# An attention and feed-forward kernel on one core: its thousand work items in a new order

## The chip, the cores and the metric

The kernel runs on one core of a Trainium2 chip. The metric is device time in microseconds, the median of several runs, lower is better. Profiles are of one execution each. The engines are TensorE (PE in the profile; its weight loads are PEld), VectorE (DVE), ScalarE (ACT), GpSimd (POOL) and SyncE (SP), which here only issues transfers.

## The reference

Four sequences of 768 tokens, eight heads of 64. Heads 0, 2 and 6 ("retrieval") attend causally to everything before them; the other five ("streaming") attend to the first 4 tokens and to a window of 64. Then a two-layer feed-forward block with a leaky rectifier follows.

```python
scores = scale * np.matmul(q, k.transpose(0, 1, 3, 2))
causal = rel >= 0                       # rel: query position minus key position
stream_keep = causal & (is_sink | in_win)   # sink: key < 4; window: rel < 64
a = softmax of scores, masked by causal (retrieval) or stream_keep (streaming)
x = (a @ v), heads side by side         # 3072 tokens x 512
h = x @ w_in                            # 512 -> 2048
g = np.maximum(h, 0.0) + alpha * np.minimum(h, 0.0)
out = g @ w_out                         # 2048 -> 512
```

## The kernel before

**Segments and items.** A segment `n` (0 to 15) is one pair of heads of one sequence: sequence `n // 4`, pair `n % 4` of (2,6), (1,5), (0,4), (3,7). The feed-forward block works in tiles `t` (0 to 7): even ones are the first 512 tokens of a sequence, odd ones the other 256. All work is cut into a thousand named items, and the list `ORDER` says in which order they are emitted. Every engine, and every queue that issues transfers, executes its own instructions strictly in that order; an instruction that waits holds up all behind it on its engine. So the list is the whole schedule: no planner stands between it and the chip.

**Names.** Of segment `n`, head `h` (0 or 1), part `m`:

- `Lq`, `Lk`, `Lv`: loads of q, k and v, issued on SP (the first half of `Lk0` on ScalarE's queue). There are four buffers of each, so `Lk10` must wait for the cast of segment 6.
- `Cq`, `Ck`, `Cv`: casts to bf16; on GpSimd for segments 0 to 5, on ScalarE or VectorE later (`Cq6` and `Cq7` on ScalarE, `Cv6` on VectorE). `Cv` of a streaming pair in the first sequence has two small copies behind the cast.
- `T`, `t`: transposes of q and k by TensorE (L361, L363) and their copy out of PSUM to `qT`, `kT` (L368, L386 to L394), segments 0 to 7. From segment 8 on, `Dq` and `Dk` do both with transposing transfers on SP.
- `S`, `s`, `m`: score matmuls (L413; L423 and L430 from segment 4 on), exp by ScalarE (L469, L517 to L523), mask by VectorE (L479, L528, L531). The first sequence adds its masks on TensorE instead (L462, L501). Some `m` items hold no instruction.
- `A`, `a`: products with v (L552), normalized by VectorE (L562, L563). `X`, `x`: the transpose of that into `xT`, on TensorE for segments 0 to 3 and 15, else as a transposing transfer on SP (L571).
- `P`, `p`, `g`: up-projection of a tile (L597), `relu(-h)` by ScalarE (L602), the leaky rectifier by VectorE (L609). Some `P0` items are cut in three, so that they can start before all four segments are there.
- `O`, `o`: a quarter of a down-projection (four matmuls, L617), its copy by ScalarE (L623) and the store (L627, on GpSimd's queue for tiles under 6, else SP). The very last 128 tokens are cut by columns: `L0` to `L2` and `l0` to `l2` (L636, L645, L646).
- `wi0` to `wi7` and `wo0` to `wo3`: pieces of the two weights, issued by GpSimd (L692, L696). `wi0` and `wi1` together hold the first 512 columns of `w_in`, `wi6` and `wi7` the last.
- `warm0` to `warm8`: filler matmuls on zeros (L687), 32, 3, 14 and then 4 each. The rest (`id`, `kz`, `sz`, `nms`, `ns`, ...) fill constants and masks.

**Banks.** PSUM has eight banks. An item that needs one takes the free one that was given back longest ago, as the list is read; so the order also decides whose copy a matmul waits for.

**Bursts.** From segment 4 on, score matmuls are collected while only items follow that may stand beside them (casts, copies, exps, loads). When another item comes, the collected ones are issued. If both heads have at least 576 columns, the matmuls of the two heads alternate, each with its 64 rows of keys and queries (L430), and run beside each other on the two halves of the array; otherwise they are issued one by one with all 128 rows, of which half are zeros (L423):

```python
if min(columns) < SPLIT:                 # 576
    for x in burst:
        nc.tensor.matmul(*x[3:6], start=True, stop=True)
else:
    ...
```

Of the kernel before, what the change touches and what calls it, by code (L numbers as in the profile page):

```python
# [14 lines left out]
busy zero La id warm0 kz3 Lq0.0 sz1 vz2 nms nmr so1 vz0 Lq0.1 Lk1 warm8 warm5 warm3 kz1 qz0 one Lq1 Lk0 Ck0.0 Cq0.0  # L15
Tq0.0 tq0.0 Tk0.0 qz kz0 kz2 idf warm2 Lk2 tk0.0 Ck1.0 Ck1.1 Cq0.1 Tk1 S0.0.1 s0.0.1 Tq0.1 S0.0.0 Cq1 warm7 Lv0 tk1.0
sz2 vz1 vz3 Tq1 Lq2 Ck0.1 S0.0.2 s0.0.0 tk1.1 Tk0.1 Ck2.1 tq1 S1.1.0 s0.0.2 Ck2.0 warm4 tq0.1 nz0 s1.1.0 Cq2 tk0.1 Cv0
Lk3 S0.1.0 kfz0 Lv1 vo ro0 Ck3.1 s0.1.0 Lq3 Ck3.0 wi1 wi0 Cq3 sz0 S1.0.0 so2 Al s1.0.0 so0 al S0.1.1 s0.1.1 Lv2 Tq2
Tk2 tk2.1 tk2.0 S0.1.2 S1.0.1 A0.0 s0.1.2 a0.0 Cv1 A0.1 a0.1 Cv2 s1.0.1 tq2 S1.1.1 nz1 Tk3 S2.0.1 tk3.0 s1.1.1 S2.0.2
X0 s2.0.1 x0 wi6 s2.0.2 wi7 Lv3 Lq5 Tq3 tk3.1 S2.0.0 wi5 m4.0.2 warm6 S2.1.0 A1.0 a1.0 Lk4 s2.0.0 A2.0 S2.1.1 A1.1  # L20
a2.0 tq3 s2.1.0 a1.1 S3.0.0 s2.1.1 s3.0.0 A2.1 a2.1 S3.1.1 X1 S3.0.1 s3.0.1 Lk5 wi4 kfz2 Cv3.0 Cq5 Lk7 wi2 X2 Ck4.0
s3.1.1 S3.1.0 x1 P0.0.0 x2 P0.0.1 A3.0 P0.1.0 P0.1.1 Lk6 Lq4 Lq6 Ck4.1 kfz3 nr Cv3.1 s3.1.0 A3.1 Lv7 Lv5 Lq7 Ck5.0 wi3
# [824 lines left out]
```

## Time and profile before

| | before |
|---|---|
| median of 3 runs | 229.27 us (229.27 to 230.81) |
| the profiled execution | 229.83 us |
| its span, first to last instruction | 228.0 us |
| TensorE busy | 222.4 us, 2005 matmuls |
| VectorE, ScalarE, GpSimd busy | 151.6, 139.6, 45.8 us |
| transfers | 37.39 MB, mean 164 GB/s |

The page names for each group its line, engine, what it writes and reads, how often it occurs, and the mean time of one. "Idle before" is time that the engine stood ahead of such instructions, with what ended most of it. Matmuls are pipelined: their busy times overlap, so the distance from one start to the next says what each costs. The chain that ended last goes back from the last instruction to what released each step.

### The profile page before, as it was taken

The page shows a single profiled execution, that of the slowest core. Times are in us where ns is not written, and L with a number is a line of the kernel's source. Part 1 is how long each engine was busy: PE and PEld are TensorE (multiplying, and loading weights), DVE is VectorE, ACT ScalarE, POOL GpSimd, SP SyncE. Part 2 cuts the span into 40 slices and gives each one's busy share as a digit, 9 for nine tenths or more (in the row PEclk, how much of TensorE's full clock was granted, in tenths as well). Part 3 has the DMA queues.
Part 4 walks back from the last instruction along what each step waited for, and adds up shares of the span by engine and source line. Part 5 has one row for each costly group of instructions (what it writes and reads, how often), then busy time and mean ns, then how long its engine had stood idle before and what let it go on. Part 6 is the DMA issues. An engine that isn't in the chain of part 4 may idle for free.

```text
span 228.0 us, 5239 instructions
## 1 busy us (share of the span) xinstructions
PE 222.4 (98%) x2005; PEld 135.9 (60%) x2005; DVE 151.6 (66%) x395; ACT 139.6 (61%) x284; POOL 45.8 (20%) x91
## 2 busy tenths in 40 slices
PE   8999999999999999999999999999999999999994
PEld 8789876563455656555556455556556555664454
DVE  7769849966389816899699219987586535966000
ACT  2689559999799128477994136787594236563311
POOL 6769996101130001000400001000110110000000
PEclk9999999999999999999999999999999999999999
DMA  6999999999998798989969899995821420000213
GB/s 190 313 229 210 286 223 262 206 197 241 206 287 142 132 204 227 172 192 181 254 153 199 194 266 146 218 166 107 132 93 38 116 95 0 0 4 0 88 66 123
DMA packets 95417, 37.39 MB, mean 164 GB/s; under 512 B 82440, under 2 KB 93600, under 8 KB 95392
## 3 DMA queue, kind: packets, MB, share of 16 engines
q1 hardware_dynamic: 89136, 27.73, 61.2%
q0 software_dynamic: 5792, 8.93, 17.1%
q10 hardware_dynamic: 464, 0.40, 0.5%
q8 instruction: 15, 0.25, 0.5%
q14 instruction: 10, 0.08, 0.2%
HBM read 27.71 MB, written 6.29 MB: 149 GB/s over the span
## 4 chain that ended last, share of the span: by engine, by line
PE 92%; ACT 3%; DVE 2%; issue 1%; DVEq 0%; ACTq 0%
PE P L597 35%; PE P L617 34%; PE P L552 7%; PE P L430 4%; PE P L687 3%; PE P L413 2%; PE P L363 2%; PE P L636 2%; ACT neg L602 1%; PE P L501 1%; DVE kT L392 1%; PE P L423 1%; PE P L577 1%; ACT kT L392 1%; ACT eS L523 1%
## 5 line engine op out<-in xcount | busy, mean ns | idle before, releaser
L609 DVE SCALAR_TENSOR_TENSOR g<-neg,oma,P 128x256 bf16<-128x256 f32 (+1 forms) x128 | 71.0, 608 | 35.9 <-ACT neg L602 35.5
L597 PE MATMUL P<-xT,w_in_b 128*128 128x512 bf16 (+1 forms) x512 | 86.5, 326 | 0.0
L617 PE MATMUL P<-w_out_b,g 128*128 128x512 bf16 x368 | 85.4, 379 | 0.0
L602 ACT ACTIVATE neg<-P 128x512 f32<-128x512 f32 x96 | 54.4, 600 | 27.2 <-PE P L597 22.6
L597 PEld LDWEIGHTS <-w_in_b 128*128 128x128 bf16 x512 | 49.5, 98 | 31.7 <-DVE g L609 0.2
L617 PEld LDWEIGHTS <-g 128*128 128x128 bf16 x368 | 33.8, 98 | 37.2 <-issue 1.2
L469 ACT ACTIVATE eR<-P 128x448 bf16<-128x448 f32 (+4 forms) x63 | 37.1, 636 | 5.4 <-PE P L430 2.3
L623 ACT COPY ot<-P 128x512 f32<-128x512 f32 x23 | 13.8, 602 | 37.8 <-PE P L617 32.9
L627 POOL DMA_DIRECT2D out_dram<-ot x18 | 10.3, 571 | 113.2 <-ACT ot L623 113.0
L517 ACT ACTIVATE eS<-P 128x352 bf16<-128x352 f32 x45 | 21.0, 493 | 3.7 <-PE P L430 3.7
L563 DVE TENSOR_TENSOR xn<-P,rcp 128x448 bf16<-128x448 f32 (+1 forms) x32 | 19.5, 608 | 1.1
L528 DVE TENSOR_TENSOR eS<-eS,ms_near 128x352 bf16<-128x352 bf16 x45 | 14.3, 334 | 4.4 <-ACT eS L517 4.2
L479 DVE TENSOR_TENSOR eR<-eR,mr_near 128x128 bf16<-128x128 bf16 (+5 forms) x54 | 12.1, 252 | 4.0 <-ACT eR L469 4.0
L430 PE MATMUL P<-qT,kT 64*128 64x176 bf16 (+13 forms) x181 | 11.7, 251 | 0.3 <-DVE g L609 0.3
L430 PEld LDWEIGHTS <-kT 64*128 64x128 bf16 x181 | 7.2, 94 | 7.6 <-issue 6.8
L413 PE MATMUL P<-qT,kT 128*128 128x192 bf16 (+14 forms) x68 | 11.3, 251 | 0.3 <-ACT eS L523 0.3
L552 PE MATMUL P<-vb,eS 128*128 128x65 bf16 x260 | 11.0, 193 | 0.4 <-DVE eS L528 0.4
L552 PEld LDWEIGHTS <-eS 128*128 128x128 bf16 x260 | 9.7, 97 | 2.9 <-DVE eS L528 0.6
L562 DVE RECIPROCAL rcp<-P 128x7 f32<-128x7 f32 (+1 forms) x32 | 6.3, 198 | 7.1 <-PE P L552 6.9
L552 PE MATMUL P<-vb,eR 128*128 128x65 bf16 x276 | 10.1, 192 | 0.0
L552 PEld LDWEIGHTS <-eR 128*128 128x128 bf16 x276 | 9.4, 97 | 1.2
L645 DVE COPY ot<-P 128x128 f32<-128x128 f32 x1 | 0.3, 292 | 14.3 <-PE P L636 14.3
(95 smaller groups left out, 175.5 us busy)
## 6 DMA issues: line engine op xcount, KB each, us to landing
out_dram<-ot POOLq DMA_DIRECT2D x18, 256.0 KB, 3.6
kf<-in_k_dram SPq DMA_DIRECT2D x21, 192.0 KB
qf<-in_q_dram SPq DMA_DIRECT2D x18, 192.0 KB
vf<-in_v_dram SPq DMA_DIRECT2D x14, 196.0 KB
qf<-in_q_dram SPq DMA_DIRECT2D x7, 384.0 KB
vf<-in_v_dram SPq DMA_DIRECT2D x12, 192.0 KB
w_in_b<-in_moe_w_in_dram POOLq DMA_DIRECT2D x8, 256.0 KB, 9.7
w_out_b<-in_moe_w_out_dram POOLq DMA_DIRECT2D x4, 512.0 KB, 13.4
```

The lines of the kernel that those rows point to most:

```text
L413: nc.tensor.matmul(to, keys, queries, start=True, stop=stop)
L430: nc.tensor.matmul(to, keys[own], queries[own], start=True, stop=True)
L469: nc.scalar.activation(ebuf[n, hh][:, lo:hi].rearrange("p (x c) -> p x c", x=len(parts)), P[:, got[0]:got[0] + len(parts), 0:(hi - lo) // ...
L517: nc.scalar.activation(slots, sc[:, 0:352].rearrange("p (s c) -> p s c", c=176), AF.Exp, scale=scale)
L528: nc.vector.tensor_tensor(slots, slots, ms_near[:, 0:2, :] if m == 0 else ms_near[:, 1:3, :], op=ALU.mult)
L552: nc.tensor.matmul(pav[:, i, :], e[:, o:o + 128], vv[:, j, hh, 0:D + 1], start=(m == 0), stop=(m == len(terms) - 1))
L563: nc.vector.tensor_tensor(xn[n][:, 0:nt, D * hh:D * hh + D], pav[:, :, 0:D], rcp.to_broadcast([128, nt, D]), op=ALU.mult)
L597: nc.tensor.matmul(psg[:, w * i:w * (i + 1)], w_in_b[:, c, 128 * fb:128 * (fb + 1)], xT[:, c, o:o + w], start=(x == 0), stop=(x == 3))
L602: nc.scalar.activation(neg[t, f], bank(held["P", t, f][0]), AF.Relu, scale=-1.0)
L609: nc.vector.scalar_tensor_tensor(g_buf[t % 2][:, fb, 0:w], neg[t, f][:, c], oma[:, fb:fb + 1], bank(got[0])[:, c], op0=ALU.mult, op1=ALU.add)
L617: nc.tensor.matmul(bank(held["O", t, s][0]), g_buf[t % 2][:, f, 128 * s:128 * (s + 1)], w_out_b[:, f, :], start=(f == 0), stop=(f == 15))
L623: nc.scalar.copy(ot, bank(got[0]))
```

## The change

Only the list `ORDER` changes. It holds the same items, each once, in another order over its whole length; no function and no constant is touched. Which score matmuls are collected into one burst, and which banks the items take, follow from the new order. Of the 56 lines on each side the diff below shows the opening, the middle around segments 4 to 7, the end of the second batch in the new list, and the end.

```diff
--- before
+++ after
 ORDER = """
-busy zero La id warm0 kz3 Lq0.0 sz1 vz2 nms nmr so1 vz0 Lq0.1 Lk1 warm8 warm5 warm3 kz1 qz0 one Lq1 Lk0 Ck0.0 Cq0.0
-Tq0.0 tq0.0 Tk0.0 qz kz0 kz2 idf warm2 Lk2 tk0.0 Ck1.0 Ck1.1 Cq0.1 Tk1 S0.0.1 s0.0.1 Tq0.1 S0.0.0 Cq1 warm7 Lv0 tk1.0
-sz2 vz1 vz3 Tq1 Lq2 Ck0.1 S0.0.2 s0.0.0 tk1.1 Tk0.1 Ck2.1 tq1 S1.1.0 s0.0.2 Ck2.0 warm4 tq0.1 nz0 s1.1.0 Cq2 tk0.1 Cv0
-Lk3 S0.1.0 kfz0 Lv1 vo ro0 Ck3.1 s0.1.0 Lq3 Ck3.0 wi1 wi0 Cq3 sz0 S1.0.0 so2 Al s1.0.0 so0 al S0.1.1 s0.1.1 Lv2 Tq2
-Tk2 tk2.1 tk2.0 S0.1.2 S1.0.1 A0.0 s0.1.2 a0.0 Cv1 A0.1 a0.1 Cv2 s1.0.1 tq2 S1.1.1 nz1 Tk3 S2.0.1 tk3.0 s1.1.1 S2.0.2
-X0 s2.0.1 x0 wi6 s2.0.2 wi7 Lv3 Lq5 Tq3 tk3.1 S2.0.0 wi5 m4.0.2 warm6 S2.1.0 A1.0 a1.0 Lk4 s2.0.0 A2.0 S2.1.1 A1.1
-a2.0 tq3 s2.1.0 a1.1 S3.0.0 s2.1.1 s3.0.0 A2.1 a2.1 S3.1.1 X1 S3.0.1 s3.0.1 Lk5 wi4 kfz2 Cv3.0 Cq5 Lk7 wi2 X2 Ck4.0
-s3.1.1 S3.1.0 x1 P0.0.0 x2 P0.0.1 A3.0 P0.1.0 P0.1.1 Lk6 Lq4 Lq6 Ck4.1 kfz3 nr Cv3.1 s3.1.0 A3.1 Lv7 Lv5 Lq7 Ck5.0 wi3
...
-m4.1.3 A5.0 a5.0 X5 s4.1.1 A4.0 s7.0.0 s7.1.1 Lk11 Lq8 s7.0.1 a4.0 s6.0.5 near1 m7.0.0 m7.1.1 m4.1.0 O1.1.0 S7.1.0
-S6.0.4 S7.0.2 S4.1.5 S6.0.1 S7.1.2 S6.1.1 O1.1.1 Cv6 s7.1.0 O1.0.0 s4.1.5 m7.0.1 s6.1.1 m4.1.5 m6.1.1 s7.1.2 m6.1.0
-s7.0.2 m7.0.2 S6.0.2 S4.1.2 S6.1.2 S6.0.0 s6.0.4 s4.1.2 s6.0.1 s6.1.2 O1.0.1 m6.0.5 m7.1.0 m4.1.1 m4.1.4 m7.1.2 m6.1.2
...
-O0.0.1 O0.0.2 O1.0.2 m10.0.2 O1.0.3 O0.0.3 o0.0 X4 X6 a7.1 a7.0 X7 P2.9 P2.3 p2.9 P3.4 Ck9 Cq9 g2.9 P2.14 p2.14 g2.14
-Cq8 p3.4 Lq10 Lq11 Dk8.0 P2.10 p2.10 Dk9.1 o1.0 p2.3 g2.3 g3.4 Dk8.1 P3.2 P3.14 P3.12 P2.8 Dq8 P2.1 P3.8 o1.1 p3.2
...
-g3.0 p2.15 g2.7 g2.15 S8.0.0 p2.12 g2.12 Ck11 p3.6 S9.0.2 P2.6 p2.6 g3.6 s8.0.0 p2.4 g2.4 g2.6 s9.0.2 p3.8 P3.10 g3.8
-p3.10 O3.0.0 O2.0.0 S8.1.5 s8.1.5 O3.0.1 O2.0.1 g3.10 m8.0.0 Cv8 S8.1.3 S9.0.0 S8.0.3 S9.1.1 S8.0.1 S9.1.0 s8.1.3
-s9.1.0 s8.0.1 s9.0.0 s8.0.3 m8.0.3 m8.0.1 O2.0.2 O2.0.3 o2.0 Dk10.1 Lv9 m9.0.0 Cv9 m8.0.5 Dk11.0 m9.1.0 m9.0.2 S8.0.4
...
-p6.14 g6.14 g7.12 O6.3.3 o6.3 O6.0.2 O6.1.2 O6.1.3 o6.1 O6.0.3 o6.0 O6.2.0 O6.2.1 O6.2.2 O7.0.1 O7.0.2 O6.2.3 o6.2
-m12.0.2 g7.14 L2 l2 O7.0.3 o7.0 L0 L1 l1 warm1 l0
+id vo kz3 busy warm0 sz0 vz0 zero nms warm5 nz1 nmr sz1 Lq0.0 so1 kz1 Lk1 qz0 Lq1 Cq0.0 Lq0.1 sz2 Ck1.0 Lk0 Ck0.0
+Tq0.0 La Ck1.1 Cq1 Cq0.1 tq0.0 Lk2 Ck2.0 Tk0.0 kz0 Lv0 warm2 Ck0.1 ro1 Ck2.1 Tk1 tk0.0 S0.0.1 S0.0.0 Tq1 Lq2 tk1.0 Cv0
+s0.0.1 Cq2 Tq0.1 Lk3 tk1.1 nz0 Lq5 Lq3 m4.1.2 so2 warm4 S0.0.2 tq0.1 warm7 warm6 Tk0.1 m8.1.2 s0.0.0 tq1 qz S1.1.0 Tk2
+Ck3.1 Ck3.0 s0.0.2 vz1 Lv1 tk0.1 vz3 S0.1.0 idf s1.1.0 Cq3 kz2 tk2.1 warm3 S1.0.0 warm8 s0.1.0 Al al tk2.0 s1.0.0
+S0.1.1 vz2 Lv2 Tq2 s0.1.1 S0.1.2 s0.1.2 wi1 wi0 tq2 A0.0 a0.0 S1.1.1 A0.1 s1.1.1 Lv3 S1.0.1 a0.1 Cv1 Cq5 Cv2 Tk3 tk3.1
+s1.0.1 wi7 Lk4 S2.0.1 s2.0.1 S2.0.2 so0 Lk5 X0 x0 Tq3 S2.0.0 wi6 tk3.0 s2.0.2 A1.0 A1.1 a1.0 S2.1.1 wi5 wi4 Cv3.0
+s2.0.0 a1.1 Tq5 ro0 S2.1.0 tq3 A2.0 a2.0 s2.1.1 S3.1.1 Ck4.0 wi2 s2.1.0 A2.1 s3.1.1 S3.0.0 Ck4.1 S3.0.1 X1 s3.0.1 one
...
+P0.9 Tk6 kfz1 p0.4 g0.4 O0.2.0 Cv5 p0.9 P0.5.0 tk6.1 m5.1.1 tk6.0 P1.8 P0.5.1 P0.5.2 p0.5 g0.9 S5.1.0 g0.10 s5.1.0
+Ck7.1 g0.5 Tq6 tq6 S4.0.2 m5.1.0 s4.0.2 p0.8 g0.8 P1.6 p1.6 g1.6 O0.1.0 Tk7 tk7.1 O0.3.0 O0.3.1 Cv6 p1.8 tk7.0 O0.1.1
+S5.0.2 S5.1.2 S4.0.4 S6.1.0 s5.1.2 s5.0.2 s6.1.0 s4.0.4 m4.0.1 O0.1.2 O0.1.3 m4.0.4 Cv4 o0.1 near0 g1.8 S4.1.0 S4.1.4
+S4.0.3 S4.0.0 Cq7 O0.2.1 s4.1.4 O0.2.2 m5.1.2 Tq7 s4.0.0 s4.0.3 m4.0.5 tq7 m4.0.3 O0.2.3 o0.2 A5.1 a5.1 Lk8 S5.0.1
+s5.0.1 s4.1.0 O0.3.2 O0.3.3 o0.3 Lk9 S4.1.1 S6.0.4 S7.1.1 S6.0.5 Lq9 S4.1.3 S4.1.5 S6.0.0 near2 m4.1.4 s7.1.1 m5.0.1
...
+m4.1.1 m12.0.2 s7.0.2 Lk11 S6.1.2 s6.1.2 m6.1.2 S4.1.2 O1.0.0 m6.0.0 m7.0.2 S6.0.2 s4.1.2 Dk8.1 O1.0.1 m6.1.0 s6.0.1
+m6.0.1 s7.1.2 m7.1.2 A4.1 a4.1 S7.0.0 A6.1 a6.1 s6.0.2 Lq8 A6.0 a6.0 S7.0.1 s7.0.1 X4 A7.1 m7.0.1 O1.1.2 O1.1.3 X6
+m8.0.2 s7.0.0 m7.0.0 A7.0 a7.1 O0.0.0 O1.0.2 O1.0.3 O0.0.1 O0.0.2 O0.0.3 a7.0 Ck9 X7 P2.10 P2.14 o0.0 Cq8 Dk8.0 Ck10
...
+X10 O3.1.3 a11.1 X11 O2.1.2 Lq13 Cq13 O2.2.1 O2.2.2 O2.2.3 Lq14 Dq12 O2.1.3 o2.1 m12.1.2 P4.13 P4.6 P4.12 p4.13 P5.14
...
+O6.1.0 P7.8 O6.1.1 P6.11 g7.14 g6.12 P6.8 p7.12 p7.8 g7.8 p6.11 g6.11 O6.2.0 p6.8 O6.0.0 p6.14 g6.8 O6.0.1 O6.0.2
+g7.12 p7.2 g7.2 L0 O7.0.0 P6.15 p6.15 L2 l2 g6.14 O7.0.1 O7.0.2 g6.15 O6.1.2 O6.1.3 O6.0.3 o6.0 O7.0.3 O6.2.1 l0
+O6.2.2 o6.1 O6.2.3 o6.2 o7.0 O6.3.0 O6.3.1 O6.3.2 O6.3.3 o6.3 L1 l1 warm1
 """.split()
```

## The prediction

> **What bounds the kernel now.** I read three things in this order: busy time by engine, the chain that ended last, then the timeline of TensorE for each place where it stood.
>
> ```profile
> PE 222.4 (98%) x2005; PEld 135.9 (60%) x2005; DVE 151.6 (66%) x395; ACT 139.6 (61%) x284; POOL 45.8 (20%) x91
> PE 92%; ACT 3%; DVE 2%; issue 1%; DVEq 0%; ACTq 0%
> ```
>
> TensorE is the bound, and 92% of the chain lies on it. Busy time can't say how close it is to full, since matmuls overlap; the starts can. Back to back, matmuls start 216 ns apart at 512 columns, 109 at 256, 56 at 128, 82 at 192 and 29 at 65. I put these intervals on every matmul of the old order. The sum is 217.4 us. TensorE in fact runs from 1.07 us to 225.0, which is 223.9 us, so 6.5 us are something other than streaming. That is all a new order can touch, beside the streaming that it changes itself. It stands in these places:
>
> - 2.4 us: the first 47 or so matmuls start 106 ns apart instead of 56, up to 6.2 us.
> - 1.4 us: gaps between 6.5 and 15 us, the longest 0.63 (before 10.92, for kT) and 0.33 (before 12.97, for an exp).
> - 0.35 us before 25.95 (an exp frees its bank late).
> - 1.39 us later: 0.15 at 41.6, 0.19 at 52, 0.45 before 54.98 (a bank, VectorE's g), 0.61 before 64.59 (a mask).
> - about 0.9 us in crumbs that any order will have.
>
> ```profile
> 10.92 0.49 PE L363 MATMUL P<-ident,g 128*128 128x128 bf16 x6 [0.47 <-DVE kT L394]
> 25.95 0.24 PE L413 MATMUL P<-qT,kT 128*128 128x192 bf16 x1 [0.19 <-ACT eS L523]
> 54.98 0.36 PE L430 MATMUL P<-qT,kT 64*128 64x320 bf16 x4 [0.29 <-DVE g L609]
> 64.59 0.45 PE L552 MATMUL P<-vb,eS 128*128 128x65 bf16 x9 [0.45 <-DVE eS L528]
> ```
>
> The bracket gives the idle time and its releaser; it is shorter than the gap in starts because ends are modelled. After 72 us there is no gap over 0.13 us.
>
> **The change part by part.** No instruction is added but for how score matmuls are grouped; below, the "stream time" of an item is the sum of intervals on TensorE up to it, and its "offset" is real time less stream time.
>
> *1. Score matmuls that run in pairs: +0.56 us.* Scores from segment 4 on are collected and issued as a burst; when both heads have at least 576 columns, they are issued as 64-row matmuls that run beside each other (L430), else one after another (L423). I applied the rule to both lists. Old: 17 paired bursts whose longer halves hold 20088 columns, and 4424 columns unpaired. New: 14 with 16752, and 10480 unpaired, in 50 matmuls instead of 23. A paired burst took 0.417 ns for each column of its longer half (1248 columns: 520 ns) and 0.215 us beside that (0.096 before it, about 0.118 in it; median of 16). So: 27232 - 24512 = 2720 columns more, 1.13 us; three bursts fewer, -0.645; 27 more matmuls at 2.5 ns, +0.07. Nothing hides this; TensorE is full there.
>
> *2. The opening.* 36 filler matmuls run ahead of the first transpose instead of 44 (8 x 106 ns = 0.85 us saved), and the 8 stand later among work at 56 ns (0.45 us, inside the new stream time of 218.0). The two fills between the kT copies (0.5 us on VectorE from 9.22) go, and K of segment 0 is issued first on ScalarE's queue, 0.45 us earlier. By these alone TensorE would run about 1 us ahead at 13 us.
>
> *3. What is late next: the queue of GpSimd.* The first value product of segment 1 (A1.0) needs Cv1. Old:
>
> ```profile
> 16.20 1.41 POOL L692 DMA_DIRECT2D w_in_b<-in_moe_w_in_dram  x2
> 17.60 0.85 POOL L315 CAST g<-qf 128x768 bf16<-128x768 f32 x1
> 18.36 0.95 POOL L348 CAST vb<-vf 128x896 bf16<-128x896 f32 x1
> 19.38 0.63 POOL L306 COPY vb<-vb 4x192 f32<-4x192 f32 x2
> ```
>
> It ends at 20.0 and A1.0 starts at 21.09, stream time 16.17, offset 4.92. New: GpSimd does Cq3 first, then both weight issues, then Cv1, then Cq5, then Cv2. Cq3 waits for Lq3, which now has Lq5 ahead of it on SP in place of Lv1. The completions of Lk3 came at 14.76, Lv1 1.38 later, Lq3 1.14 after that. Lq5's own took 0.75 (25.23 to 25.98), while Lq6, of the same size, took 2.56 (40.52 to 43.08). I take 1.0, since Lq3 and Lq1 beside it took about 1.1. Lq3 then lands at 14.76 + 1.0 + 1.14 = 16.9; Cq3 ends at 17.7, the two weight issues (1.41) at 19.1, Cv1 (1.6 with its two copies) at 20.7. A1.0 starts there with stream time 15.52: offset 5.2, against 4.92. Cv2 follows at 22.7, and A2.0 (stream time 17.61) asks at 22.8. So the lead of part 2 is lost in this queue. At the first up-projection (P0.0.0) old offset is 5.4; new 5.2 plus 0.1 for crumbs. **-0.1 us**, from -0.3 (Lq5 0.75) to +1.4 (2.56).
>
> *4. Weights.* wi1 and wi0 are issued 2 us later than before (17.7 and 18.4, against 16.2 and 17.0; wi0 landed at 25.04), so wi0 lands near 26.6, and P0.0.0 asks at 26.9. wi7 and wi6 go out 0.5 us later (landed 30.25 and 32.03); P0.15 asks at 27.4 + 5.3 = 32.7, one microsecond earlier than before. Both are just in time: 0 to 0.5 us. I take 0.1.
>
> *5. The middle.* The places of 1.39 us are gone in the new list: g of P0.x frees banks with over 0.2 us to spare, and A5.1's mask has time. I listed, for every operation of ScalarE and VectorE, the matmul that waits for it, and set the operations queued up to it against the TensorE work in between (ScalarE instructions back to back start 0.11 us before the last one's end, VectorE's 0.08). In the old list 24 lack time by this count, in the new one 8. The worst of those: 13 instructions of ScalarE from s6.0.0 to s6.0.2, 6.3 us, between stream times 59.8 and 67.0 less two handovers, short by 0.5 us at A6.0. The count is pessimistic: it gave 1.15 us for an old place near 172 us, where TensorE stood for none. New waits: Cq7 stands in ScalarE's queue behind o0.1 (real time about 58.3) and needs Lq7, which now comes behind Lv5, Lv6 and Lv4 instead of Lv7 and Lv5; it landed at 57.75 and will land near 59. ScalarE stands 0.7 us, and behind it stand s4.1.4 and s4.0.0, whose banks are asked for 1 to 2 us later. Cv6 waits likewise on VectorE for Lv6, some 2 us, ahead of g1.8, which has 3 us to spare. Bounds for all of it: 0 to 2.0 us; I take 0.8. **1.39 goes, 0.8 comes: -0.6 us.**
>
> *6. Batch ends and the tail.* After the last value product of batches 1 and 2, the old order has 7 and 8 groups of output matmuls (0.86 us each) to cover the transposes to xT, the new one 6 and 6; batch 3 has 3 in both. The first, the tightest, needs 1.2 us of VectorE and 2.6 from issue to landing (X7: 78.67 to 81.3) against 5.2: covered. At the very end o6.3's copy and its 256 KB now start 0.9 us before the last matmul; that size took 0.8 us of packets (223.76 to 224.56), so the last small store may queue for 0.1 to 0.2. **+0.1 us.**
>
> **Sum.** 0.56 - 0.1 + 0.1 - 0.6 + 0.1 = about 0.1 us more to nothing, on a span of 228.0. The profiled execution took 229.83 us, 1.8 around the span; the median of the runs is 229.27, 0.56 below. I carry the difference over, not the absolute time, and lean to the pessimism of the count in part 5: **229.2 us**, unchanged. About 1% (2.3 us) is what a measurement of this kernel can tell from no change.
>
> **A rule weighed.** The trace shows matmuls of 128 columns 106 ns apart until 6.2 us and 56 after:
>
> ```profile
> 1.07 4.88 PE P L687 x44
> 6.85 0.89 PE P L687 x14
> ```
>
> The Trainium skill, "TensorE: Matmul & The Clock Gate", section "What's actually happening", says that the array runs at half clock until a free-running activity window of about 3.4 us has been busy. By that page a TensorE that now stands between 5.6 us and the arrival of K could miss its window and rise one later. The rise here, 5.1 us after the first matmul, agrees with that; a miss no run here shows. What a miss would give is the third rival, priced from rows.
>
> **Rivals.**
>
> *Slower: the input chain.* Everything after A1.0 hangs on when Lq3 lands, one for one. At Lq6's price Lq3 lands 1.5 us later and A1.0 with it; the weights behind it on GpSimd go out as much later, and if one of wi6 and wi7 comes one piece late (1.78 us between their landings), P0.15 stands for that: up to +3.2 us, 232.4; at half of it 230.8. It decides once Lq3 lands after about 17.2. For it: GpSimd's queue is at 92% from 13 to 26 us, and DMA engines are busy throughout. Against: Lq3 replaces no larger transfer ahead of it. 0.22.
>
> *Faster: few new waits.* If ScalarE's places cost as little as the old ones did, parts 4 and 5 give 0.2 instead of 0.9 and part 3 its lower end: 229.2 - 0.9 = 228.3; for over 1% the opening would have to keep its lead as well, against the queue of part 3. 0.18, a third of it beyond 1%.
>
> *The slow start lasts longer.* If the intervals stay at 106 ns until 9.6, TensorE's work of 6.2 to 9.6 us, about 2.9 us, doubles; the lead of 1 us and the waits there take most, leaving 1 to 1.5: 230.5. 0.08.
>
> Forecast 0.52. Faster by over 1%: 0.07; within 1%: 0.75; slower by over 1%: 0.18 (most of the first rival's upper half, and both waits of part 5 at their bound). The range takes in the second rival and most of the first: 227.8 to 231.7.
>
> **What would show it.** L423 with 50 matmuls and L430 with 154; GpSimd with Cq3, two weight issues, then Cv1, and A1.0 (first L552 of 13) within 0.3 us of Cv1's end; no gap before kT's transposes near 10.9; gaps, if any, at 58 to 76 us by ScalarE. I am wrong if TensorE stands over 1 us anywhere after 30 us, or if A1.0 doesn't follow Cv1.

## The result and the profile after

The new order took 231.06 us (median of 21 runs, 229.8 to 234.0), the old one beside it 229.29 us (21 runs, 228.38 to 231.76): ratio **1.007, 95% interval 1.0049 to 1.009**. The ratio leaves out three slow executions of the new order, the longest three of the 21 (233.44 to 234.0 us). Two later series gave 1.0133 (1.0094 to 1.0173) and 1.0093 (1.0058 to 1.0128). The new order is some 2 us slower. The prediction had it unchanged.

The profiled execution of the new order was a long one (234.0 us, span 232.3), so a second (232.39, span 229.6) and a third profile (span 230.0) of the same kernel stand beside it below. Here is the first: the line of the page on the engines, the shares of the chain that ended last, and, from the list of groups, the three groups of matmuls that the prediction names.

```profile
PE 223.4 (96%) x2005; PEld 136.8 (59%) x2005; DVE 151.6 (65%) x395; ACT 139.4 (60%) x284; POOL 45.8 (20%) x91
PE 44%; issue 24%; DMA 15%; SPq 10%; POOL 5%; DVE 1%; POOLq 0%; DVEq 0%
L597 PE MATMUL P<-xT,w_in_b 128*128 128x512 bf16 (+1 forms) x512 | 89.8, 330 | 2.2 <-DMA w_in_b<-in_moe_w_in_dram 2.2
...
L430 PE MATMUL P<-qT,kT 64*128 64x176 bf16 (+12 forms) x154 | 9.7, 250 | 0.0
...
L423 PE MATMUL P<-qT,kT 128*128 128x176 bf16 (+9 forms) x50 | 8.4, 254 | 0.0
```

The group of L597 in the old order, for comparison:

```profile
L597 PE MATMUL P<-xT,w_in_b 128*128 128x512 bf16 (+1 forms) x512 | 86.5, 326 | 0.0
```

L597 has 2.2 us of idle time for the weights now and had none. L423 has 50 matmuls and L430 154, as counted. TensorE was on 92% of the chain before and is on 44% now. Followed back from the end, the chain stays on TensorE as far as 126.8 us; there it turns to a load of K, and from that to a long stretch in which GpSimd's queue stood:

```profile
92.61 26.31 issue
...
120.28 4.84 DMA kf<-in_k_dram
```

In the second and third profile the chain leaves TensorE at the same place. So there are two stands to explain, this one and the one for the weights. The waits of TensorE, by what they waited for (line, releaser, total, times, longest), in the first profile:

```profile
PE P L597 <- DMA w_in_b<-in_moe_w_in_dram: 2.2, 1, 2.2
...
PE P L552 <- DVE eR L479: 0.9, 1, 0.9
```

They are one stand each. The timeline of TensorE has the first at P0.15, which needs `wi6` and `wi7`; the later of the two landed at 35.06, where it had landed at 32.03 in the old order. The windows behind it (length, busy time of the engines, granted clock, share of the DMA engines, GB/s) show what came after:

```profile
32.66 0.38 PE L597 MATMUL P<-xT,w_in_b 128*128 128x512 bf16 x1
35.20 5.00 PE L597 MATMUL P<-xT,w_in_b 128*128 128x512 bf16 x22 [2.16 <-DMA w_in_b<-in_moe_w_in_dram]
```

```profile
32.00:35.05 3.05, 1.03 (x6) 0.29 (x3) 1.35 (x2) 1.21 (x3) 1.38 (x3) 1.00 1.16 252
35.05:38.46 3.41, 3.26 (x12) 1.71 (x13) 0.79 (x2) 0.60 (x1) 3.08 (x11) 0.50 1.20 218
38.46:41.87 3.41, 3.41 (x26) 2.38 (x25) 2.47 (x6) 2.94 (x6) 3.35 (x10) 1.00 1.18 237
```

TensorE stood until 35.2, and then the clock was granted at 0.50 for 3.41 us, which cost 1.6 us more, by the offset from P0.15 to P0.14. The second stand, the one on the chain, is far later, at A8.1. Its mask m8.1.4 stands on VectorE behind Ck13, the cast of K of segment 13, and that stood for its load. VectorE, TensorE and GpSimd of the new order, first profile:

```profile
125.20 0.63 DVE L334 CAST natk<-kf 128x896 bf16<-128x896 f32 x1 [1.30 <-DMA kf<-in_k_dram]
125.74 0.22 DVE L479 TENSOR_TENSOR eR<-eR,mr_near 128x128 bf16<-128x128 bf16 x1
```

```profile
126.83 0.54 PE L552 MATMUL P<-vb,eR 128*128 128x65 bf16 x12 [0.88 <-DVE eR L479]
```

```profile
118.94 0.54 POOL L627 DMA_DIRECT2D out_dram<-ot  x1 [26.33 <-ACT ot L623]
119.63 1.30 POOL L242 DMA_DIRECT2D kf<-in_k_dram  x2 [0.15 <-issue]
```

The load that is late is a small one. Of Lk13, the 4 sink rows alone are issued on GpSimd's queue (`nc.gpsimd if n == 13`), and there the new list has them behind the store of o3.0, which waited 26.33 us for ScalarE's copy. So they went out at 119.63 and landed at 125.1. The old list had `Lk13` ahead of `o3.0`:

```profile
111.60 1.50 POOL L242 DMA_DIRECT2D kf<-in_k_dram  x2 [0.22 <-issue]
```

```profile
121.11 0.62 DVE L334 CAST natk<-kf 128x896 bf16<-128x896 f32 x1
```

They went out at 111.60, and Ck13 ran at 121.11 without a wait.

Where the time went, by the offset of the prediction (real time less the sum of TensorE's own intervals up to an item):

| | P0.0.0 | stand at P0.15 | offset behind it | A9.0 (111 to 114 us) | stand at A8.1 | last matmul |
|---|---|---|---|---|---|---|
| old order | 5.39 | 0 | 5.42 | 7.11 | 0 | 7.50 |
| new, first profile | 5.48 | 2.3, then half clock | 9.41 | 9.69 | 1.0 | 11.08 |
| new, second | 5.75 | 0.24 | 6.02 | 7.15 | 0.9 | 8.40 |
| new, third | 6.06 | 1.5 | 7.83 | 8.05 | 0.8 | 8.85 |

To the offsets of the new order 0.56 us of longer streaming is to be added. So three things make the loss: pairing, the weights at P0.15, which differ from execution to execution, and the load ahead of A8.1. The experiments are to show which of them the time is really made of.

### The profile page after: what moved, and what is told of

It reads as the page before. It is cut to its first block, busy times and chain, and to the rows that moved or that the text cites. A ratio compares the mean times of both kernels' runs of the same rounds, so it can differ in the third digit from the quotient of the medians.

```text
span 232.3 us, 5246 instructions
## 1 busy us (share of the span) xinstructions
PE 223.4 (96%) x2005; PEld 136.8 (59%) x2005; DVE 151.6 (65%) x395; ACT 139.4 (60%) x284; POOL 45.8 (20%) x91
## 4 chain that ended last, share of the span: by engine, by line
PE 44%; issue 24%; DMA 15%; SPq 10%; POOL 5%; DVE 1%; POOLq 0%; DVEq 0%
PE P L617 20%; PE P L597 18%; DMA kf<-in_k_dram 10%; SPq L242 5%; SPq L239 4%; PE P L552 3%; DMA vf<-in_v_dram 3%; DMA qf<-in_q_dram 2%; POOL out_dram L627 2%; PE P L636 2%; PE P L430 1%; SPq L246 1%; POOL g L328 1%; POOL w_in_b L692 1%; PE P L423 0%
## 5 line engine op out<-in xcount | busy, mean ns | idle before, releaser
L597 PE MATMUL P<-xT,w_in_b 128*128 128x512 bf16 (+1 forms) x512 | 89.8, 330 | 2.2 <-DMA w_in_b<-in_moe_w_in_dram 2.2
L609 DVE SCALAR_TENSOR_TENSOR g<-neg,oma,P 128x512 bf16<-128x512 f32 (+1 forms) x128 | 71.6, 609 | 28.3 <-ACT neg L602 26.6
L602 ACT ACTIVATE neg<-P 128x512 f32<-128x512 f32 x96 | 55.8, 610 | 27.1 <-PE P L597 20.3
L597 PEld LDWEIGHTS <-w_in_b 128*128 128x128 bf16 x512 | 49.8, 99 | 34.6 <-issue 4.1
L469 ACT ACTIVATE eR<-P 128x448 bf16<-128x448 f32 (+4 forms) x63 | 36.6, 629 | 4.4 <-PE P L462 2.2
L528 DVE TENSOR_TENSOR eS<-eS,ms_near 128x352 bf16<-128x352 bf16 x45 | 15.5, 353 | 2.1 <-ACT eS L517 2.0
L479 DVE TENSOR_TENSOR eR<-eR,mr_near 128x128 bf16<-128x128 bf16 (+5 forms) x54 | 10.4, 225 | 4.0 <-ACT eR L469 4.0
L552 PE MATMUL P<-vb,eR 128*128 128x65 bf16 x276 | 10.3, 193 | 1.2 <-DVE eR L479 0.9
L430 PE MATMUL P<-qT,kT 64*128 64x176 bf16 (+12 forms) x154 | 9.7, 250 | 0.0
L430 PEld LDWEIGHTS <-kT 64*128 64x128 bf16 x154 | 5.8, 94 | 5.5 <-issue 5.1
L423 PE MATMUL P<-qT,kT 128*128 128x176 bf16 (+9 forms) x50 | 8.4, 254 | 0.0
```

The lines of the kernel that those rows point to most:

```text
L430: nc.tensor.matmul(to, keys[own], queries[own], start=True, stop=True)
L469: nc.scalar.activation(ebuf[n, hh][:, lo:hi].rearrange("p (x c) -> p x c", x=len(parts)), P[:, got[0]:got[0] + len(parts), 0:(hi - lo) // ...
L528: nc.vector.tensor_tensor(slots, slots, ms_near[:, 0:2, :] if m == 0 else ms_near[:, 1:3, :], op=ALU.mult)
L552: nc.tensor.matmul(pav[:, i, :], e[:, o:o + 128], vv[:, j, hh, 0:D + 1], start=(m == 0), stop=(m == len(terms) - 1))
L597: nc.tensor.matmul(psg[:, w * i:w * (i + 1)], w_in_b[:, c, 128 * fb:128 * (fb + 1)], xT[:, c, o:o + w], start=(x == 0), stop=(x == 3))
L602: nc.scalar.activation(neg[t, f], bank(held["P", t, f][0]), AF.Relu, scale=-1.0)
```

## The experiments

In the mixed and moved lists the line numbers are one lower where the list takes one line fewer. Times stand against runs of the old order on the same chip (229.03 to 229.35 us by series).

### The new order once more

> The changed kernel itself, for a profile without a drop of the granted clock. Theory (late weights and a late K): TensorE stands 1 to 2 us before P0.15 (L597 at about 33 us) until a w_in piece lands, and about 1 us before A8.1 (L552 at about 124 us); time 231.0, 0.7% over the kernel before. Rival (the unpaired score matmuls and crumbs): no gap over 0.5 us after 30 us, and the 1.7 us spread over the bursts.

Measured: 232.21 us, 1.0133 (1.0094 to 1.0173). In its profile P0.15 hardly stands, and TensorE stands 0.58 us for weights at P0.0.0. The profiled execution took 232.39 us, but its span is 229.6: 2.8 us lie outside the span, where 1.7 to 1.8 do in most executions, so the span is the fairer measure, 1.6 us over the old order's. Tq7 stands for ScalarE's cast Cq7 (0.55 us idle, 0.72 by the starts), as step 5 of the prediction had it; the stand at A8.1 is there.

### The weights earlier

```diff
-Cq3 ... wi1 wi0 ... Cv1 Cq5 Cv2 ... wi7
+wi1 Cq3 wi0 ... Cv1 Cq5 wi7 Cv2
```

> Only three weight issues move forward on GpSimd, into places where it stood idle: wi1 ahead of Cq3 (1.5 us earlier) and wi7 ahead of Cv2 (1.4 us earlier). Theory (P0.15 waits for wi7 and wi6): the wait shrinks by 1.0 to 1.5 us and the time falls to about 229.8. Rival (the queue of weight transfers is full, so an earlier issue lands no earlier): under 0.3 us. Rival (the wait costs nothing, as what follows was late anyway): the wait shrinks and the time stays at 231.

Measured: 231.8 us, 1.0124 (1.0094 to 1.0154). No gain. wi1 was issued at 15.69 and wi7 at 21.42, against 17.64 and 23.33 in the first profile of the new order, and P0.15 did not stand. But GpSimd's cast of V of segment 2 waited for its load until 23.81 (22.04 in the first profile; 21.26 and no wait in the second), and TensorE stood for that cast (this profile is of the slowest of the five runs):

```profile
24.80 1.53 PE L551 MATMUL P<-vb,eR 128*128 128x65 bf16 x27 [2.10 <-POOL vb L347]
```

```profile
22.50:24.97 2.47, 0.37 (x9) 0.22 (x7) 0.30 (x2) 0.81 (x1) 1.09 (x2) 1.00 1.41 184
24.97:28.38 3.41, 3.41 (x52) 3.35 (x49) 1.47 (x5) 0.49 (x1) 2.86 (x6) 0.50 1.22 238
```

The half clock came again, for 3.41 us, and cost 1.6 us here too. The Trainium skill, "DMA: Bandwidth & Descriptors", section "Issuing engines are not separate DMA queues", says that transfers run on the same DMA engines whichever engine started them. So the earlier weights may have made the input late. No run here shows that they did: in the six profiles of the new order's opening left as it was, the same cast ran at 21.26 to 23.25 us, so a part of the 23.81 at least is scatter.

### Ck13 behind the masks

```diff
-Ck13 m10.0.0 Cv11 ... m8.1.4 A8.1 ... Dk13.0
+m10.0.0 Cv11 ... m8.1.4 A8.1 ... Ck13 Dk13.0
```

> Only Ck13 moves, on VectorE, from ahead of m10.0.0 to just ahead of Dk13.0, behind the masks that A8.1 and A10.0 need. Theory (VectorE stands for Lk13 with A8.1's mask behind it): the 1 us gap before A8.1 goes, time 230.0. Rival (the slack later takes it up): the gap goes and the time falls by less than 0.3.

Measured: 230.97 us, 1.0074 (1.0046 to 1.0103). A8.1 no longer stands. The offset of the last matmul is 7.00 in its profile, which is of the fastest of its runs. Against the new order of the same series (1.0133) that is 0.6%; against the first series (1.007) it is nothing. The time alone doesn't settle it.

### Pairing undone in the old order

```diff
-    SPLIT = 576
+    SPLIT = 801
```

> The kernel before with the least size for pairing raised from 576 to 801 columns: five bursts (shorter halves 704, 800, 800, 800, 800) are issued unpaired. By the price of part 1: 3904 columns more at 0.417 ns is 1.63 us, less 5 times 0.215, so 0.55 us more, 229.8. Rival (a pair saves nothing beside its 0.215): 1.1 us less, 228.2. Rival (unpaired bursts hide in waits): unchanged.

Measured: 229.87 us, 1.0043 (1.0022 to 1.0064), 0.5 to 1.5 us for five bursts fewer in pairs. In its profile the last matmul starts at 225.48, 0.61 us later than in the old order's (224.87). Both rivals are out, and step 1 of the prediction holds: the 0.55 us expected lies inside the interval. The median, 0.84 us, is higher; whether the price is a little low is not shown.

### Old first half, new second half, and the reverse

```diff
 (the first list up to X7 of batch 1, then what is left, in the order of the other list)
+old_new: before[:X7] + rest in the order of after
+new_old: after[:X7]  + rest in the order of before
```

> The old list up to the end of batch 1 (X7), the new one behind it: the old opening, weights and bursts of segments 4 to 7, and the new batches 2 and 3. Stream time by the count: 217.6 us, 0.18 more than the old list. Theory (pairing plus the late 4-row load of K13): A8.1 again waits about 1 us near 123 us; 229.3 + 0.2 + 0.8 to 1.0 = 230.3 to 230.5, ratio 1.004 to 1.006. Rival (the loss comes from the opening, the weights and Lq7): nothing of that is left here, so 229.3 to 229.6, ratio within 1.001, and a wait at A8.1 that is made up later.

> The new list up to the end of batch 1, the old one behind it: the new opening and the new bursts of segments 4 to 7, and the old batches 2 and 3, with the 4-row load of K13 ahead of o3.0 again. Stream time 217.8 us, 0.38 more than the old list. Theory (the opening costs nothing by 111 us, as the trace of the new order has it): 229.3 + 0.4 = 229.7, ratio 1.002, no wait at A8.1; where P0.15 stands over 2 us and the clock halves, up to 2 more. Rival (the loss comes from the opening): nearly all of the new order's loss, 231 to 232, ratio 1.007 to 1.012. The two mixed lists together should give the loss of the new order if the two parts add up.

Measured: old_new 231.56 us, 1.0092 (1.0058 to 1.0126); new_old 230.4 us, 1.0056 (1.0022 to 1.0089). Both halves lose. The first has a flaw of its own: at the seam a score burst stands for a transposing transfer that neither original waits for.

```profile
90.61 0.35 PE L422 MATMUL P<-qT,kT 128*128 128x320 bf16 x2 [1.80 <-DMA qT<-natq]
```

So old_new says: 0.2 of streaming, 0.9 at A8.1 (Ck13 stood 1.12 us, until 123.64), and the rest, 1.3, is put down to the seam, which stood 1.80 us in this profile, the slowest of its seven runs. new_old has no such seam: of its 1.25 us, 0.38 is streaming and 0.9 (0.1 to 1.7) was lost ahead of X7. All its stands over 0.3 us lie in the opening. Its profile, the slowest of 12 runs, has the stand at P0.15 again, 2.41 us idle, but the clock stayed at 1.00 behind it:

```profile
36.65 0.59 PE L596 MATMUL P<-xT,w_in_b 128*128 128x512 bf16 x2 [2.41 <-DMA w_in_b<-in_moe_w_in_dram]
```

```profile
33.90:36.65 2.75, 0.34 (x3) 0.03 (x2) 1.40 (x2) 1.08 (x2) 1.78 (x4) 1.00 1.18 245
36.65:40.06 3.41, 3.41 (x24) 2.29 (x25) 1.53 (x3) 2.08 (x4) 3.02 (x13) 1.00 1.20 218
```

Why a stand of 2.16 us was followed by the half clock and one of 2.41 was not is answered below, from the times at which the clock changed.

The expectation that the opening costs nothing by 111 us rested on one profile, the second, and is wrong: over the runs the first batch in the new order costs nearly one microsecond. The 12 runs of new_old go from 229.3 to 232.5 us.

### The same with Ck13 moved, and Lk13 ahead of o3.0

```diff
-Ck13 m10.0.0 ... m8.1.4 A8.1 ... Dk13.0
+m10.0.0 ... m8.1.4 A8.1 ... Ck13 Dk13.0     (in old_new)
```

> The old list up to the end of batch 1, the new one behind it, with Ck13 moved from ahead of m10.0.0 to just ahead of Dk13.0, so that m8.1.4 no longer stands behind its wait on VectorE. Theory: only the 0.18 us of stream time are left, 229.4 to 229.5, ratio 1.000 to 1.001, and the gap ahead of A8.1 is gone. Rival (the gap at A8.1 is made up later, or it is the new opening that costs): the same time as the list without the move.

Measured: 230.33 us, 1.005 (1.0028 to 1.0071), 1.2 us below old_new. Both have the seam, and the edit touches only Ck13. In a list with the old opening the stand at A8.1 is thus worth about what the trace gives it, 0.9 us, though the two intervals just overlap.

```diff
-o3.0 ... Lk13
+Lk13 o3.0       (in the new list)
```

> The new list with one item moved: Lk13 ahead of o3.0, as it stands in the old list, so that its two 4-row transfers on GpSimd's queue are not behind the store of o3.0, which waits for ScalarE. Ck13 stays where the new list has it. Theory: the transfers are issued some 5 to 8 us earlier (old: 111.6, new: 119.6), Ck13 finds its load, A8.1 does not wait, and the time is that of the list with Ck13 moved: 1.0 to 1.3 us below the new order, ratio to the old 1.003 to 1.008. Rival (Ck13 costs VectorE at that place whether or not its load is there): A8.1 still waits 0.5 us or more and at most 0.5 us is gained.

Measured: 231.13 us, 1.0087 (1.0056 to 1.0117). The two small transfers went out at 89.66, and Ck13, at its old place, ran without a wait, as did A8.1:

```profile
120.75 0.63 DVE L333 CAST natk<-kf 128x896 bf16<-128x896 f32 x1
```

That shows the chain of the wait: o3.0's store, the sink rows behind it, Ck13, m8.1.4, A8.1. But the time is that of the new order in its first series. The runs go from 229.8 to 233.0 us, and that scatter can hide a microsecond. So of the three lists that take the stand at A8.1 away, the two with Ck13 moved are each 1.2 us below their neighbour of the same series, and this one shows no gain in its time.

### Inside the opening: Q5 back, and P1.0 first

> The new order unchanged, as the measure for the three lists beside it. Over the first two series it had spans from 227.6 to 232.3 us, half of them between 229.0 and 230.1, while the old order had half of its spans within 0.5 to 1.0 us. Expected: ratio to the old order 1.007 to 1.013, the same width, a wait at A8.1 of about 1 us, and a wait at P0.15 that differs from run to run (0.2 to 2.6 us so far).

Measured for the new order in this series: 231.49 us, 1.0093 (1.0058 to 1.0128); spans from 228.7 to 231.0 us, where the old order had half of its own between 227.2 and 227.6.

```diff
-Lq5 Lq3 Lv1 Lv2 Lv3 ... Cv1 Cq5 Cv2 wi7 wi6 ... Tq5 ... Tk4
+Lq3 Lv1 Lv2 Lv3 Lq5 ... Cv1 Cv2 wi7 wi6 Cq5 ... Tk4 Tq5
```

> The new list with the load of Q5 back behind Lv3, where the old list has it, its cast behind the issue of wi6 instead of between Cv1 and Cv2, and its transpose Tq5 behind Tk4. Theory (the input chain: Lq5 ahead of Lq3 and Cq5 in GpSimd's queue make Cv1, Cv2 and both weight issues late): Lq3 lands 0.75 to 1.0 us earlier, Cv2 starts 1.5 us earlier, wi7 and wi6 are issued 1.5 to 1.8 us earlier, A2.0 no longer stands, P0.15 stands 0.5 us or less; 0.7 to 1.2 us below the new order and a narrower width. Rival (the DMA engines are the limit, and any order of the loads only moves the wait): weights no earlier than before by 0.5 us, and the time of the new order within 0.4 us.

Measured: 235.76 us, 1.0234 (1.0179 to 1.029). The edit was a bad one. Q5 landed only at 29.1, GpSimd stood for it 6.37 us, and behind its cast stood wi5, wi4 and the cast of V3, for which TensorE stood 4.2 us:

```profile
29.14 0.82 POOL L314 CAST natq<-qf 128x768 bf16<-128x768 f32 x1 [6.37 <-DMA qf<-in_q_dram]
```

What it does show is that the pieces that P0.15 needs did come earlier: wi7 was issued at 21.55 (23.33, 22.54 and 23.57 in the three profiles of the new order), the later of wi7 and wi6 landed at 32.32 (35.06, 33.26 and 34.63), and no matmul stood for weights. They were the only weights on the way then, since wi5 and wi4 still stood behind Q5. So the theory held for the weights, and the wait moved to V3 and became longer.

```diff
-P0.15 p0.15 Lk6 g0.15 wo0 kfz3 P1.0
+P1.0 P0.15 p0.15 Lk6 g0.15 wo0 kfz3
```

> The new list with P1.0 (whose weights wi0 and wi1 are there) ahead of P0.15, the order that the old list has: the first use of wi6 and wi7 is asked for 0.87 us of TensorE later. Theory (weights late at P0.15): its wait is shorter by 0.87 us, or gone where it was less; 0.3 to 0.9 us below the new order. Rival (P0.15 stands only in rare executions, and the opening's loss lies ahead of it): within 0.2 us of the new order.

Measured: 231.73 us, 1.0106 (1.0064 to 1.0149): no gain alone. In its profile P0.15 stood 0.25 us; A8.1 stood 1.1. The move also brings a stand of its own, for ScalarE's `relu` (L601): 0.45 us at 37.56. It is there again, 0.53 us at 38.03, in the list with three moves below.

```diff
 Q5 back, P1.0 first, and:
-o3.0 ... Lk13       Lv4 ... Lq7
+Lk13 o3.0           Lq7 Lv4
```

> The new list with all four waits undone: Lq5, Cq5 and Tq5 back, P1.0 ahead of P0.15, Lk13 ahead of o3.0, and Lq7 ahead of Lv4 so that Cq7 doesn't wait. Theory: what is left is the pairing, 0.56 us of stream time by the count and 0.8 by the run with five bursts unpaired, so 229.7 to 230.2, ratio 1.002 to 1.004. If the waits in the middle of the old order (1.39 us) were a loss there and are gone here, 228.6 to 229.2, ratio 0.997 to 1.000. Rival (waits only move): 230.5 or more.

Measured: 235.18 us, 1.0194 (1.0133 to 1.0254). It has the bad edit in it and says nothing on the rest.

### The three waits mended, without the bad edit

```diff
-P0.15 ... P1.0      o3.0 ... Lk13       Lv4 ... Lq7
+P1.0 P0.15          Lk13 o3.0           Lq7 Lv4
```

> The new list with P1.0 ahead of P0.15, Lk13 ahead of o3.0 and Lq7 ahead of Lv4; Lq5, Cq5 and Tq5 stay where the new list has them. Theory: the waits at A8.1 (about 1 us) and Tq7 (0 to 0.7) go, the one at P0.15 shrinks; what stays is the pairing (0.56 to 0.8) and the opening up to P0.0.0 (0.4): 230.0 to 230.6, ratio 1.004 to 1.006, against 1.009 for the new order. Rival (the scatter of the opening takes what the mending gives): 231.0 or more.

Measured: **229.99 us, 1.0036 (1.0007 to 1.0066)**. The waits of TensorE in its profile are down to these four, the first of which is the start:

```profile
PE P L686 <- DVE busy L287: 1.4, 1, 1.4
PE P L596 <- ACT neg L601: 0.5, 1, 0.5
PE P L412 <- DVE qT L287: 0.5, 1, 0.5
PE P L551 <- POOL vb L305: 0.2, 1, 0.2
```

With three moves of one item each the loss is 0.64 us (0.2 to 1.5), where the new order lost 1.8, 3.2 and 2.4 us in its three series. What stays has the size of the pairing. Of the three, two were tried alone and showed no gain beyond the scatter; the third, Lq7, was not tried alone. Together they do show one, as far as series can be compared: the new order was not run again in this one, and its first series (1.0049 to 1.009) overlaps this interval.

### The weights late in the old order

```diff
-wi1 wi0 Cq3
+Cq3 wi1 wi0
```

> The old list with one item moved: Cq3 ahead of wi1 and wi0 instead of behind them, as the new list has it on GpSimd; nothing else of the opening changes. Cq3 waits for Lq3 (17.3 us), so wi1 and wi0 are issued 1.9 us later, Cv1 ends 1 us later, wi6 and wi7 are issued 0 to 0.5 us later. Theory (the weights' transfers run one behind another, so that 1.9 us at the head of their queue is 1.5 to 2 us at wi6 and wi7 too): P0.0.0 or P0.15 stands, 0.5 to 1.5 us together, and the runs scatter more; ratio 1.002 to 1.007. Rival (the landing follows each one's own issue, and the new order's waits come from its earlier demand): at most 0.3 us, ratio within 1.0015, the width of the old order.

Measured: 231.58 us, 1.0098 (1.0066 to 1.0129). One item moved, and the old order loses as much as by the whole new list. wi1 was issued at 17.88 instead of 16.20. But the way is not the expected one. P0.15 does not stand at all; TensorE stands for Cv2 (0.68 us, at A2.0), a little for the weights at P0.0.0 (0.20), and longest at A3.1 for a copy on VectorE:

```profile
PE P L551 <- DVE vb L305: 1.3, 1, 1.3
```

That copy, 4 rows of 192 elements, took 0.37 us in the old order. Here are VectorE and GpSimd at that place, in this list:

```profile
26.65 1.24 DVE L342 CAST vb<-vf 128x448 bf16<-128x448 f32 x1
27.93 2.56 DVE L305 COPY vb<-vb 4x192 f32<-4x192 f32 x1
```

```profile
27.97 0.97 POOL L327 CAST natm<-kf 128x384 bf16<-128x384 f32 x2
28.87 0.21 POOL L287 MEMSET kf<- 128x128 f32 x1
29.03 1.27 POOL L658 TENSOR_SCALAR_AFFINE_SELECT mr_near<-one 128x1248 bf16<-128x1248 bf16 x1
30.24 0.61 POOL L327 CAST natm<-kf 128x384 bf16<-128x384 f32 x1
```

GpSimd works without a break from 27.97 (its spans are rough), and the copy ends 0.2 us behind its long mask instruction. In the old order the copy ran at 27.17, ahead of most of that stretch:

```profile
27.17 0.37 DVE L306 COPY vb<-vb 4x192 f32<-4x192 f32 x1
```

The Trainium skill, "SBUF — State Buffer", section "Who interferes with whom", says that VectorE and GpSimd share one pair of ports to SBUF, by an exclusive lock. By that page the copy can have waited for GpSimd. The next list tests it by shortening GpSimd's stretch. The late copy does not need the moved item, though: in the profile of old_new_ck13, whose opening is the old one and where Cv2 stood 1.36 us for its load, the copy took 2.55 us beside the same stretch, and TensorE stood 1.62 us for it.

```diff
 (with Cq3 ahead of wi1 as above)
-kfz3 nr ... Ck5.0 wi3
+kfz3 ... Ck5.0 wi3 nr
```

> The old list with Cq3 ahead of wi1 and wi0, as in the list that lost 2.2 us by it, and GpSimd's mask instruction nr (1.27 us) moved from behind kfz3 to behind wi3, so that GpSimd's unbroken stretch beside VectorE's 4-row copy (Cv3.1) is shorter by 1.27 us. In that list the copy took 2.56 us in place of 0.37 and ended 0.19 us behind nr. Theory (VectorE's copy stands as long as GpSimd works without a break): the copy takes 1.0 to 1.6 us, A3.1 stands 0.2 to 0.6 in place of 1.44, and the time is 0.8 to 1.2 us below that list: ratio to the old order 1.004 to 1.006. Rival (the copy waits for something else): 2.5 us again and ratio 1.009 or more.

Measured: 230.75 us, 1.0059 (1.0036 to 1.0081), 0.83 us below. The copy took 0.68 us, less than expected, and A3.1 stood no longer:

```profile
27.70 0.68 DVE L305 COPY vb<-vb 4x192 f32<-4x192 f32 x1
```

```profile
PE P L596 <- DMA w_in_b<-in_moe_w_in_dram: 1.2, 1, 1.2
```

Instead P0.0.0 stood 1.2 us for its weights, wi1 and wi0. The later of them landed at 27.79; in the list before it had landed at 27.22, and TensorE had already lost 0.68 us at A2.0. So the theory of late weights is right in kind, at P0.0.0: moved 1.7 us back in GpSimd's queue, the first two pieces cost TensorE 1.2 us in one profile and 0.2 in the other. For wi6 and wi7 at P0.15 neither list shows it. And the 2.56 us belong to GpSimd's work: with the mask instruction out of the stretch, 1.9 of them went. The copy did not have to wait for all that was left of it, two casts and a fill from 27.74 to 28.90; how the two engines take turns is not shown.

### The old order's own waits

```diff
-m5.1.0 ... m5.0.0 ... m4.0.4 m5.1.1 A5.1        tk7.1 g0.4 Cv5 p1.6
+m5.1.0 m5.1.1 ... m5.0.0 ... m4.0.4 A5.1        p1.6 tk7.1 g0.4 Cv5
```

> The old list with two items moved: m5.1.1 directly behind m5.1.0 on VectorE, so that A5.1 finds its mask (its wait at 64.59 was 0.61 us), and p1.6 ahead of tk7.1 on ScalarE, so that the burst at 54.98 finds its bank (0.45 us). It tests the gain that the prediction gave to the old order's waits. Theory (they are losses, and nothing later takes them back: after 72 us there is no gap): 0.8 to 1.1 us less, 228.1 to 228.4, ratio 0.995 to 0.9965. Rival (given back at the next wait, by ScalarE's or VectorE's queue, or by tk7.1 being 0.6 us later): ratio 0.998 to 1.001.

Measured: 228.97 us, 0.9987 (0.996 to 1.0014). Both stands are gone from the trace: A5.1 runs through, 13 matmuls without a bracket,

```profile
63.19 0.55 PE L551 MATMUL P<-vb,eS 128*128 128x65 bf16 x13
```

and the offset between P0.15 and A9.0 grows by 0.91 us, where it grew by 1.69 in the old order's profile. The median is lower by 0.38 us; the interval runs from 0.9 us less to 0.3 more and has 1 inside.

```diff
 (with the two moves above)
-kfz3 nr ... Ck5.0 wi3
+kfz3 ... Ck5.0 wi3 nr
```

> The old list with its two waits mended (m5.1.1 earlier, p1.6 ahead of tk7.1) and nr behind wi3, so that an execution in which Cv3.1 comes late no longer stands behind it. Theory: the typical execution as without the last move (228.97), the upper tail shorter; ratio 0.996 to 0.999. Rival (what is mended is given back): 1.000 or more.

Measured: 229.01 us, 0.9981 (0.9959 to 1.0004). Its slowest of 12 runs is 229.76, the old order's of 20 is 230.71. It may be the best version by 0.3 us; the measurement doesn't settle that.

## Why the prediction was wrong

By its own sign the prediction was wrong: TensorE stood 2.16 us after 30 us. Two terms failed: the 0.1 us of step 4 for the weights, which measured about 1.3, and a wait that step 5 left at nothing, the load of Ck13, which measured 0.8 to 1.0.

**Step 1, pairing, +0.56:** right. The count of matmuls is exact. Five bursts unpaired cost the old order 0.98 us (0.5 to 1.5), and the mended new list, with no stand over 0.53 us behind its start, is 0.64 us slower than the old order.

**Step 2, a lead of 1 us at 13 us:** wrong in size. The first transpose of k (Tk0.0) starts 0.4 to 1.1 us earlier (5.23, 5.95 and 5.68 against 6.35), but S1.1.0, which has the same stream time in both lists (6.98), starts at 11.62, 11.76 and 12.11 against 11.25: the wait for the first loads and casts comes instead of the fillers. In the third profile Tq1 stands 1.0 us for the cast of Q1. The lead was never there.

**Step 3, GpSimd's queue:** right in the first profile. Cq3 ran at 16.86 (16.9 was forecast), A1.0 at 20.31 (20.7).

**Step 4, the weights, "just in time", 0.1:** this step failed. Six profiles have this opening and P0.15 at this place; it stood 2.3, 0.24, 1.5, 0.6, 0.5 and 2.6 us, 1.3 on average, and once the half clock cost 1.6 more. The step let wi6 and wi7 be issued 0.5 us later and land as much later. In six profiles of the old order's opening the later of the two landed at 31.1 to 32.8 us, in these six at 33.3 to 36.5, on average 2.6 us later: 1.5 of it is the later issue, and 1.1 is a longer way from issue to landing (10.3 us for 9.2), whose cause is not shown. By 34 us 1483 to 1663 KB of w_in were in with the old opening, and 1147 to 1359 KB with the new. And a margin of nothing is not worth 0.1 us on average: where the landing scatters by 3 us, early arrivals give nothing back and late ones cost in full.

This is the first rival, which was given 0.22. Its own condition, Lq3 after about 17.2 us, was met in two of the six: in the third profile Lq3 landed at 17.69, in new_old at 18.42, and P0.15 stood 1.5 and 2.6 us. In the other four Lq3 landed at 16.5 to 17.0 and P0.15 stood 2.3, 0.24, 0.6 and 0.5 us: there the weights alone were late. The step also says that wi1 and wi0 go out 2 us later; by its own figures it is 1.5.

**Step 5, the middle, -0.6:** half right. The old waits are gone, and TensorE did not stand at A6.0, where the count had put the worst. Cq7 stood for Lq7 and cost TensorE 0.72 us in one profile of three and next to nothing in the others. In the two profiles without that wait the offset grows by 0.2 to 0.3 us from behind P0.15 (and the half clock) to A9.0, against 1.69 in the old order. But the list of operations that the step worked from timed ScalarE's and VectorE's own instructions and not their loads. Ck13's load was outside it, on a queue that the prediction walked through only up to 26 us. That is a term of +0.8 to 1.0 us that the sum does not have.

**Step 6, the tail:** right. From A12.0 to the last matmul the offset grows by 0.16 us in the new order and 0.18 in the old.

**The sum:** with 1.3 for the 0.1 of step 4, 0.9 more in step 5 and the rest as it stood, 0.1 becomes 2.2 us. Measured were 1.8, 3.2 and 2.4 in the three series. That the rest fits is in part luck. At P0.0.0 the new order is 0.1 to 0.7 us behind in the three profiles, where step 3 had it 0.1 ahead; between P0.15 and A9.0 it gains 1.4, 0.6 and 1.5 us, where step 5 had 0.6. The two misses cancel. The forecast also took 1% for what a measurement can tell from no change; the 21 runs on each side gave an interval 0.4% wide.

The rule of the Trainium skill that was weighed ("TensorE: Matmul & The Clock Gate", section "What's actually happening"), a start of the fast clock one window later, did not decide anything: the clock rose at 4.3 and 6.7 us in the first two profiles of the new order, at 6.2 in the old.

What stays open: why the weights take longer to land in the new opening and scatter so much; how much each of the three moves of the mended list gives by itself; and whether the mended old order beats the old one.

## What to carry to other kernels

- A transfer that arrives "just in time" in one trace is a cost: take the landing times of several executions, and book the mean of what comes late, not the difference of two medians. Here 0.1 us was booked, and six profiles had 1.3 on average.
- A queue that works without a break passes any delay on to all behind it, and not where one looks. One cast moved ahead of two weight issues cost 2.2 us, by three waits, and P0.15, where the wait was expected, did not stand.
- When a list is reordered, walk every queue to its end, the seldom used ones above all. A few rows of a load sat behind a store that waited 26 us, three engines away from the matmul that paid.
- Single repairs can drown in the scatter of another fault. Two of three moves showed nothing alone, and the three together took most of the loss away; the traces had named all three.

## What the runs showed of the hardware

- A VectorE copy of 4 rows took 0.25 us in profiles where GpSimd did nothing beside it, 0.37 in the old order, and 2.56 us beside an unbroken stretch of GpSimd work of 2.3 us that began with it; its cast of 128x448 elements took 1.24 us there, 0.86 in the old order and 0.42 in the first profile of the new. The copy waited across several GpSimd instructions, not one.
- The granted clock changed only at steps of 3.41 us, counted from its first rise: at 4.33, 35.05 and 38.46 us in the first profile, 9 and 10 steps on. What counts is how long TensorE stood within one such window, not how long the stand was:

| profile | window (us) | TensorE stood in it | clock in the next |
|---|---|---|---|
| w_early | 21.56 to 24.97 | 2.10 | 0.50 |
| new order, first | 31.64 to 35.05 | 2.01 | 0.50 |
| new order, second (the end) | 225.11 to 228.52 | 1.98 | 0.50 |
| old_new | 88.75 to 92.16 | 1.80 | 1.00 |
| new_old | 32.36 to 35.77 | 1.58 | 1.00 |
| new_old | 35.77 to 39.19 | 0.88 | 1.00 |

The stand of 2.41 us in new_old was longer than the one of 2.16 in the first profile, but a boundary cut it in two. In the 17 profiles that hold the clock, every window at full clock with 1.80 us of standing or less was followed by full clock, and every one with 1.98 or more by half. A window already at half clock had to be fuller: with 0.91 us of standing in lq5_back the half clock stayed for another window. Where the boundaries lie differs between executions of one kernel (the first rise came at 4.3 and at 6.7 us in two profiles of the new order), so whether a stand of some 2 us costs 1.6 us more is luck. The Trainium skill, "TensorE: Matmul & The Clock Gate", section "HAM oscillation — how this bites in real kernels", puts the bound at idle gaps of about 3.4 us; the length of the slow stretch agrees with its window, the bound does not: 1.98 us in one window was enough here.

- The landing of a weight piece scatters: the same piece, issued at 23.1 to 25.1 us in six profiles, landed at 33.3 to 36.5.
